# Moving the small tasks of the next tiles to other steps in the first two blocks of a fused state-space and FFN kernel

## The chip, the cores and the metric

One core of one Trainium2 chip runs the whole kernel. The metric is the device time in microseconds (us) of one execution. A difference under about 0.3% (1.4 us) can't be told from no change here.

## The reference

A sequence of 2048 tokens with 448 channels, float32 throughout. A condition vector gives six rows of 448 numbers; two layer norms are shifted and scaled by them, and both branches are gated by them.

```python
mod = (_silu(c) @ w_mod).reshape(c.shape[0], 6, 1, -1)
sa, ca, ga, sb, cb, gb = (mod[:, 0], mod[:, 1], mod[:, 2], mod[:, 3], mod[:, 4], mod[:, 5])
h = _layernorm(x, axis=-1) * (1 + ca) + sa
x = x + ga * _A_ref(h, ...)          # causal convolution along the tokens, kernel K from (A, B, C, dt), plus h * Dskip
h = _layernorm(x, axis=-1) * (1 + cb) + sb
x = x + gb * _B_ref(h, w_gate, w_up, w_down)   # (silu(h @ w_gate) * (h @ w_up)) @ w_down, 448 -> 1792 -> 448
```

## The kernel before

**Tiling.** The 2048 tokens are 16 tiles of 128, taken in 8 blocks of two tiles. Block b runs the FFN of its two tiles in 14 steps, one for each slice of 128 of the 1792 hidden channels. While it does so, the other engines prepare the two tiles of block b + 1: convolution branch, second norm, and turning the result so that channels lie on partitions. What is not ready when step 13 ends holds up the next block.

**A step f** (function `ffn`). TensorE (PE) multiplies the block's turned input (`hhi` and `hlo`, a float32 value in a high and a low part) with the gate and up weights of slice f (`gu`, also high and low): 42 pairs of matmuls on the two halves of the array. Shortly before the last pair comes `point(f)`: half of the down products of slice f - 2 and half of those of slice f - 1 (operands `wdh`, `wdl` and `phi`, `plo`, or `wd` and `p` in plain float32), and, if the table says so, a part of the convolution of a coming tile. Then ScalarE (ACT) makes `p` = silu(gate) (line 792), VectorE (DVE) multiplies with up (line 804), and ACT and DVE make `phi` (812) and `plo` (813) of it for the down products. In step 0 of a block PE reads the first four seventh-slices ("LOW") of `hhi` first; they are split from the turned tiles by ACT line 267 and DVE line 268.

**Block 0** has more to do: the weights come in for the first time. In each of its steps the SyncE queue (SP) loads gate and up of a later slice into `raw` (line 108, three buffers) and the down weights into `rawd` or `wd` (line 117), ACT and DVE split gate and up into `gu` (134, 136) and down into `wdh`, `wdl` (819, 124). For the slices 4, 6, 8, 10 and 12 (`WHOLE`) the down weights stay unsplit in block 0 and are split in block 1 (122, 124).

**The tasks.** What is done for the next tiles is cut into small tasks, one letter each, with the tile's number in the block, 0 or 1. The table `PLANS` writes them out by hand, one string for block 0, one for block 1, one for the blocks in between, one for the last but one, one for the last. Steps are parted by `;`. A task with `+` is put after the multiplication of line 804 and ahead of `phi`; one without stands at the end of the step, ahead of the split of `gu` for step f + 2; `A` and `B` go into `point(f)` on PE. Each engine runs its instructions in the order in which they are written.

The tasks that matter here: `a` h from the first norm (DVE 214, 216); `b` h times two rows (1002, DVE for block 0's tasks, GpSimd, called POOL, afterwards); `r` adds the row carried from the tile before (DVE 1007, 1008); `h` and `v` split it (`vh` ACT 1013, `vl` DVE 1019); `A` and `B` the two halves of the convolution's matmuls (operands `vh`, `vl`, `v`); `c` h times the skip row and `p` its addition to x (POOL 1024, 1027); `e` takes the carried row (ACT 1051, DVE 1052) and copies it to partition 0 by a DMA (1053); `E` adds the convolution to x (DVE 1058, 1059); `u`, `w` sums for the second norm on ACT (190, 194, with POOL 191 between them), or `m` the same on DVE (170, 171); `M` the inverse root on POOL (199, 200); `X`, `Y` the second norm (DVE 223, 225); `T` transposes blocks of 32 x 32 on DVE (255) and writes the tile to DRAM by four DMAs (257, buffer `xd`); `U` reads it back turned, by two DMAs (261, into the buffers of `raw`); `l`, `k` the last two operations of the former block's sums (DVE 840, 841); `L` loads the x tile of the block after next (91); `W4` to `W12` split the whole down weights; `o`, `O` and `d`, `R` the statistics of the first norm; `G` two matmuls with their sum for the gate row (748, 749).

The names are read by this loop in `steps`:

```python
for f, names in enumerate(plan.split(";"), -2 if b == 0 else 0):
    for name in names.split():
        n = name.lstrip("+")
        ...
        if k in "AB":
            todo.setdefault((f, "pe"), []).append((st[k], nx[q[0]]))
        else:
            todo.setdefault((f, "+") if n != name else f, []).append((of[k], q))
```

Of the kernel before, what the change touches and what calls it, by code (L numbers as in the profile page):

```python
# [34 lines left out]
ADDED = ()  # L35
WHOLE = (4, 6, 8, 10, 12)
PLANS = (
# [1131 lines left out]
```

## Time and profile before

| | before |
|---|---|
| median of 3 runs | 465.16 us (464.55 to 465.99) |
| the profiled execution's own time | 466.29 us |
| its span from first to last instruction | 464.5 us |
| busy: PE, DVE, ACT, POOL | 447.6, 294.2, 157.5, 102.7 us |
| mean granted PE clock | 1.000 |

The profiled execution took 1.79 us more than its span, and 1.13 us more than the median of the runs. All positions are us from the start of the span. Block 0 begins at 35.08, block 1 at 92.61, block 2 at 146.44, block 3 at 198.50. A timeline row reads: start, duration, engine, line, operation, output<-inputs, count, and in brackets the idle time of the engine before it and what ended that. Durations of PE rows overlap, so lengths of PE work are read from the starts.

### The profile page before, as it was taken

How to read it: one execution, taken by the hardware profiler on the slowest of the kernel's cores; microseconds unless marked ns; L12 is line 12 of the kernel's file. 1: busy time of each engine (PE TensorE's matmuls, PEld its weight loads, DVE VectorE, ACT ScalarE, POOL GpSimd, SP SyncE). 2: the span in 40 equal slices, each digit the busy share in tenths (PEclk: the TensorE clock that was granted, in tenths of full speed). 3: DMA queues.
4: the chain of work that ended last, by engine and by line, in shares of the span. 5: the costliest groups of instructions: out<-in, count | busy, mean ns of one | idle time of the engine just before them, and what ended most of it. 6: DMA issues, size and time to landing. Idle time of an engine off the chain costs nothing.

```text
span 464.5 us, 14489 instructions
## 1 busy us (share of the span) xinstructions
PE 447.6 (96%) x6335; PEld 425.9 (92%) x6335; DVE 294.2 (63%) x600; ACT 157.5 (34%) x385; POOL 102.7 (22%) x127
## 2 busy tenths in 40 slices
PE   7789999899999999999999999999999999999995
PEld 4448988689899999999999999999999999999995
DVE  4889988576865666575755666565765666344324
ACT  4877554423324222332223221332223221232211
POOL 2132331033400252033301152033301161000000
PEclk9999999999999999999999999999999999999999
DMA  8953555502031102202031202202031102202001
GB/s 305 406 218 99 193 171 180 157 5 83 2 80 42 59 25 62 61 1 82 7 79 40 66 17 61 62 16 69 11 79 34 41 4 61 61 10 74 5 1 45
DMA packets 19048, 35.71 MB, mean 77 GB/s; under 512 B 3232, under 2 KB 13088, under 8 KB 18976
## 3 DMA queue, kind: packets, MB, share of 16 engines
q1 hardware_dynamic: 18336, 34.53, 23.4%
q8 instruction: 51, 0.84, 0.8%
q10 hardware_dynamic: 640, 0.18, 0.2%
q14 instruction: 21, 0.17, 0.1%
HBM read 27.76 MB, written 6.88 MB: 75 GB/s over the span
## 4 chain that ended last, share of the span: by engine, by line
PE 81%; issue 5%; DVE 5%; ACT 3%; POOL 3%; DMA 2%; SPq 0%; POOLq 0%; DVEq 0%; ACTq 0%
PE bank L766 50%; PE dn L766 27%; DMA x<-in_A_u_dram 1%; DMA raw<-xd 1%; DVE gu L136 1%; ACT gu L134 1%; PE dn L498 1%; DVE bank L804 1%; POOL m L1002 0%; POOL rsa L200 0%; POOL v L1002 0%; PE dn L872 0%; PE dn L398 0%; DVE m L223 0%; ACT phi L812 0%
## 5 line engine op out<-in xcount | busy, mean ns | idle before, releaser
L766 PE MATMUL bank<-hhi,gu 64*128 64x256 f32 x3136 | 227.4, 275 | 3.8 <-ACT hhi L267 2.3
L766 PEld LDWEIGHTS bank<-hhi,gu 64*128 64x128 f32 x3136 | 206.9, 184 | 6.8 <-ACT hhi L267 2.8
L766 PE MATMUL bank<-hlo,gu 64*128 64x256 f32 x1568 | 134.0, 275 | 0.0
L766 PEld LDWEIGHTS bank<-hlo,gu 64*128 64x128 f32 x1568 | 119.8, 184 | 0.2
L792 ACT ACTIVATE raw<-bank 128x256 f32<-128x256 f32 x98 | 37.7, 385 | 187.3 <-PE bank L766 187.3
L804 DVE TENSOR_TENSOR bank<-raw,bank 128x256 f32<-128x256 f32 x91 | 38.8, 427 | 96.6 <-ACT raw L792 96.6
L766 PE MATMUL dn<-wdh,phi 64*128 64x448 f32 x420 | 87.2, 366 | 0.4 <-ACT phi L812 0.4
L766 PE MATMUL dn<-wdh,plo 64*128 64x448 f32 x420 | 86.2, 362 | 0.0
L766 PE MATMUL dn<-wdl,phi 64*128 64x448 f32 x420 | 85.8, 359 | 0.0
L813 DVE TENSOR_TENSOR plo<-bank,phi 128x256 fp32r<-128x256 f32 x99 | 41.9, 423 | 29.5 <-ACT phi L812 29.5
L812 ACT CAST phi<-bank 128x256 fp32r<-128x256 f32 x99 | 36.9, 373 | 61.0 <-DVE bank L804 61.0
L766 PEld LDWEIGHTS dn<-wdh,phi 64*128 64x128 f32 x420 | 48.5, 184 | 3.3 <-ACT phi L812 1.5
L766 PEld LDWEIGHTS dn<-wdh,plo 64*128 64x128 f32 x420 | 48.6, 184 | 1.8 <-DVE plo L813 0.8
L766 PEld LDWEIGHTS dn<-wdl,phi 64*128 64x128 f32 x420 | 48.9, 184 | 0.9 <-issue 0.6
L1002 POOL TENSOR_TENSOR m<-m,gm 128x448 f32<-128x448 f32 x12 | 13.9, 1155 | 78.9 <-issue 43.8
L199 POOL TENSOR_SCALAR rsa<-mva 128x2 f32<-128x2 f32 (+1 forms) x10 | 5.4, 544 | 97.7 <-DVE mva L171 91.3
L199 POOL TENSOR_SCALAR rsb<-mvb 128x1 f32<-128x1 f32 x16 | 4.3, 266 | 80.2 <-DVE mvb L171 79.7
L268 DVE TENSOR_TENSOR hlo<-raw,hhi 128x512 fp32r<-128x512 f32 (+1 forms) x28 | 16.4, 622 | 3.9 <-ACT hhi L267 1.8
L1024 POOL TENSOR_TENSOR m<-m,gd 128x448 f32<-128x448 f32 x14 | 17.0, 1212 | 7.6 <-DVE v L1002 7.6
L267 ACT CAST hhi<-raw 128x512 fp32r<-128x512 f32 (+1 forms) x28 | 14.6, 566 | 3.1 <-DMA raw<-xd 3.1
L136 DVE TENSOR_TENSOR gu<-raw,gu 128x896 fp32r<-128x896 f32 x14 | 15.1, 1080 | 0.4 <-ACT gu L134 0.4
L225 DVE SCALAR_TENSOR_TENSOR m<-m,rsb,sb 128x448 f32<-128x448 f32 x14 | 13.8, 984 | 0.8
(217 smaller groups left out, 454.5 us busy)
## 6 DMA issues: line engine op xcount, KB each, us to landing
raw<-in_B_w_gate_up_dram SPq DMA_DIRECT2D x14, 448.0 KB, 3.4
raw<-xd SPq DMA_DIRECT2D x28, 224.0 KB, 3.6
xd<-m SPq DMA_DIRECT2D x56, 56.0 KB, 1.7
x<-in_A_u_dram SPq DMA_DIRECT2D x12, 224.0 KB, 2.9
rawd<-in_B_w_down_dram SPq DMA_DIRECT2D x11, 224.0 KB, 3.5
out_dram<-x SPq DMA_DIRECT2D x11, 224.0 KB, 2.0
wm<-in_w_mod_groups_dram SPq DMA_DIRECT2D x5, 448.0 KB, 8.3
wm<-in_w_mod_groups_dram SPq DMA_DIRECT2D x5, 336.0 KB, 8.2
```

Of the source, the lines that this page charges most:

```text
L136: ve.tensor_tensor(wgu[j][:, 1], w, f32(wgu[j][:, 0]), op=OP.subtract)
L199: po.tensor_scalar(rs[:, 0:n], self.mv[:, 0:n, 1], EPS, None, op0=OP.add)
L225: ve.scalar_tensor_tensor(to, to, rs, sb, op0=OP.mult, op1=OP.add)
L267: sc.copy(hi, src)
L268: ve.tensor_tensor(lo, src, f32(hi), op=OP.subtract)
L766: done.append(pe.matmul(o, w[e], r[e], start=start, stop=stop).ins)
L792: gate_ready[:] = [sc.activation(p, ps[0][:, 0:n], AF.Silu).ins.name]
L804: ve.tensor_tensor(p if whole else ps[1][:, 0:n], p, ps[1][:, 0:n], op=OP.mult)
L812: sc.copy(hi, ps[1][:, 0:n])
L813: ve.tensor_tensor(lo, ps[1][:, 0:n], f32(hi), op=OP.subtract)
L1002: en.tensor_tensor(v, h, g, op=OP.mult)
L1024: po.tensor_tensor(h, h, gd, op=OP.mult)
```

## The change

Only two strings of the table change. No instruction is added or removed.

```diff
 PLANS = (
-    """pre: s0 ; mid: t0 R0 f s1 ; a0 +g G ; b0 t1 ; r0 h0 R1 ; v0 a1 ; A0 b1 c0 ; B0 c1 e0 p0 ; r1 h1 v1 u0 w0 +E0 M0 ; X0 Y0 p1 ; A1 T0 ; B1 E1 m1 ; +M1 X1 Y1 T1 ; +U0 ; U1 e1 L0 ; L1""",
-    """d0 R0 a0 b0 d1 R1 ; +l0 r0 h0 k0 ; +l1 v0 k1 W4 ; W6 A0 a1 b1 c0 ; B0 p0 e0 E0 c1 ; W8 r1 h1 m0 M0 p1 ; +v1 X0 Y0 L0 L1 ; W10 A1 T0 U0 ; B1 E1 m1 M1 ; W12 +X1 Y1 T1 U1 ; e1 ; ; o0 ; o1 O""",
+    """pre: s0 ; mid:  t0 R0 s1 f ; +g a0 ; b0 t1 +G ; r0 R1 h0 ; v0 ; A0 b1 c0 +a1 ; B0 c1 p0 e0 ; r1 h1 v1 +E0 u0 ; M0 A1 +w0 X0 ; p1 T0 +E1 B1 +Y0 ; m1 M1 ; Y1 +X1 T1 U0 e1 ; U1 ; L0 ; L1""",
+    """ d0 R0 a0 b0 d1 ; +l0 r0 h0 +k0 ; +l1 +k1 v0 R1 W4 ; A0 a1 b1 ; E0 B0 +e0 c0 c1 ; +W6 +p0 r1 h1 m0 M0 ; +v1 X0 L0 W8 Y0 L1 ; A1 +W10 T0 ; p1 E1 U0 B1 m1 M1 ; e1 +X1 Y1 ; +T1 ; +U1 W12 ;  ; o0 o1 O""",
```

In block 0's string the third field is step 0, in block 1's the first. Block 0: `A1` moves from step 8 to 7 and `B1`, `E1` from 9 to 8; `w0` goes behind the silu of step 7, `X0` stays at the end of step 7, `Y0` goes to step 8; `M1` comes at the end of step 9 and `X1` stays ahead of `Y1` and `T1` in step 10; `U0` goes from step 11 to the end of step 10 with `e1` (12 before), `U1` from 12 to 11; `a1` from the end of step 3 into step 4, `G` from step 0 to 1.

PE, block 0, steps 7 and 8: the six rows `dn_69<-vh`, `vl`, `v` are the second tile's `A1` (rows of the order after; `gu_686` is step 7, `gu_758` step 8).

```order
L766 MATMUL dn_68<-wd_761,p 128x448 x2
L766 MATMUL dn_69<-vh,tri 128x224 x2
L766 MATMUL dn_69<-vl,tri 128x224 x2
L766 MATMUL dn_69<-v_833,tri 128x224 x2
L766 MATMUL bank<-hhi,gu_686 128x256 x2
```

Before, the same place went from the down products straight to the last pair of step 7 (there `wd_763` is what `wd_761` is now), and these rows stood one step later:

```order
L766 MATMUL dn_68<-wd_763,p 128x448 x2
L766 MATMUL bank<-hhi,gu_686 128x256 x2
L766 MATMUL bank<-hhi,gu_760 128x256 x14
L766 MATMUL bank<-hlo,gu_760 128x256 x14
L766 MATMUL bank<-hhi,gu_760 128x256 x12
```

`A1` now stands in step 7, ahead of its last pair of gate and up matmuls.

DVE, block 0, from the end of step 8 (`T0`, the transpose, is the first row) to the end of step 11, before:

```order
L255 STREAM_TRANSPOSE m_77<-m_77 128x7x2x32
L136 TENSOR_TENSOR gu_915<-raw,gu_915 128x896
L804 TENSOR_TENSOR bank<-p,bank 128x256
L124 TENSOR_TENSOR wdl_998<-rawd_79,wdh_997 128x448
L813 TENSOR_TENSOR plo<-bank,phi 128x256
L1058 TENSOR_TENSOR x_73<-x_73,dn_69 128x448
L1059 SCALAR_TENSOR_TENSOR x_73<-dn_69,tok,x_73 128x448
L170 BN_STATS stb<-x_73 128x6
L171 BN_AGGR mvb<-stb 128x2
L136 TENSOR_TENSOR gu_995<-raw,gu_995 128x896
L804 TENSOR_TENSOR p<-p,bank 128x256
```

and after, from the product of step 8 on:

```order
L804 TENSOR_TENSOR p<-p,bank 128x256
L1058 TENSOR_TENSOR x_73<-x_73,dn_69 128x448
L1059 SCALAR_TENSOR_TENSOR x_73<-dn_69,tok,x_73 128x448
L225 SCALAR_TENSOR_TENSOR m_77<-m_77,rsb,sb 128x448
L255 STREAM_TRANSPOSE m_77<-m_77 128x7x2x32
L136 TENSOR_TENSOR gu_915<-raw,gu_915 128x896
L804 TENSOR_TENSOR bank<-p,bank 128x256
L124 TENSOR_TENSOR wdl_994<-rawd_79,wdh_993 128x448
L813 TENSOR_TENSOR plo<-bank,phi 128x256
L170 BN_STATS stb<-x_73 128x6
L171 BN_AGGR mvb<-stb 128x2
L136 TENSOR_TENSOR gu_991<-raw,gu_991 128x896
```

`E1` (1058, 1059) and `Y0` (225) have moved ahead of the first tile's transpose, and out of step 9. Behind this, after the second transpose of step 10, the row of `e1`, which stood at the end of step 12, now stands ahead of the split of step 12's `gu`:

```order
 L255 STREAM_TRANSPOSE m_77<-m_77 128x7x2x32
-L136 TENSOR_TENSOR gu_1064<-raw,gu_1064 128x896
+L1052 SCALAR_TENSOR_TENSOR run<-run,dn_69 32x448
+L136 TENSOR_TENSOR gu_1068<-raw,gu_1068 128x896
 L804 TENSOR_TENSOR bank<-p,bank 128x256
```

The queue SP, block 0, from the writes of the second tile (`xd_104`) to the loads of two x tiles, before and then after:

```order
L257 DMA xd_104<-m_77 32x2x224 x4
L117 DMA rawd_81<-in_B_w_down_dram 128x448
L261 DMA raw<-xd_103 64x896 x2
L261 DMA raw<-xd_104 64x896 x2
L1053 DMA run<-run 1x16x56
L91 DMA rawd_79<-in_A_u_dram 128x448
L91 DMA rawd_80<-in_A_u_dram 128x448
```

```order
L257 DMA xd_104<-m_77 32x2x224 x4
L261 DMA raw<-xd_103 64x896 x2
L1053 DMA run<-run 1x16x56
L117 DMA rawd_81<-in_B_w_down_dram 128x448
L261 DMA raw<-xd_104 64x896 x2
L91 DMA rawd_79<-in_A_u_dram 128x448
L91 DMA rawd_80<-in_A_u_dram 128x448
```

The read back `U0` (`xd_103`) now stands ahead of the down weights of slice 13 (`rawd_81`), the copy of the carried row stands between the two, and the read back `U1` (`xd_104`) behind both.

In block 1 the string moves `W6`, `W8`, `W10` and `W12` apart (`W12` from step 9 to 11), `T1` and `U1` one and two steps later, `k0` and `k1` ahead of `plo`, `e0` ahead of `phi` in step 4, `c1` ahead of `p0`, and `E0` ahead of `p0`: on POOL the two rows 1024 now stand ahead of 1027. Both `o` tasks stand in step 13.

## The prediction

> **What bounds the kernel now.** First the page's busy rows, then the list of waits on PE, the share of PE by block, the chain of waits at the end of block 0, and from there the timelines of the engines on it.
>
> ```profile
> PE 447.6 (96%) x6335; PEld 425.9 (92%) x6335; DVE 294.2 (63%) x600; ACT 157.5 (34%) x385; POOL 102.7 (22%) x127
> ...
> PE bank L766 <- ACT hhi L267: 2.3, 1, 2.3
> PE bank L766 <- DVE gu L136: 1.1, 2, 0.7
> ```
>
> PE is busy 96% of the span. What it waits for inside the blocks is little (total, times, longest of the list's two largest rows there), above all 2.3 us on the split of the turned tile. It is the step from block 0 to block 1; the chain there, in order of time (start, length, what):
>
> ```profile
> 86.37 0.45 SPq L261
> 86.86 5.06 DMA raw<-xd
> 91.94 0.63 ACT hhi L267
> 92.61 1.63 PE bank L766 x24
> ```
>
> PE has nothing to do from 90.35 (its last row of step 13 starts at 89.85 and lasts 0.50) to 92.61, because the second half of `U1` lands at 91.92. How the SP queue, and DVE before it, came to issue it that late:
>
> ```profile
> 76.01 0.44 SPq L117 DMA_DIRECT2D rawd<-in_B_w_down_dram  x1
> 82.69 1.74 SPq L257 DMA_DIRECT2D xd<-m  x4
> 84.47 0.43 SPq L117 DMA_DIRECT2D rawd<-in_B_w_down_dram  x1
> 85.00 2.46 SPq L261 DMA_DIRECT2D raw<-xd  x4
> 89.50 1.83 SPq L91 DMA_DIRECT2D rawd<-in_A_u_dram  x2
> ...
> 72.74 0.64 DVE L255 STREAM_TRANSPOSE m<-m 128x448 f32<-128x448 f32 x1
> 75.86 0.43 DVE L804 TENSOR_TENSOR bank<-p,bank 128x256 f32<-128x256 f32 x1 [1.50 <-ACT p L792]
> 77.07 0.61 DVE L1058 TENSOR_TENSOR x<-x,dn 128x448 f32<-128x448 f32 x1
> 79.19 1.07 DVE L136 TENSOR_TENSOR gu<-raw,gu 128x896 fp32r<-128x896 f32 x1
> 80.18 0.42 DVE L804 TENSOR_TENSOR p<-p,bank 128x256 f32<-128x256 f32 x1
> 82.02 0.65 DVE L255 STREAM_TRANSPOSE m<-m 128x448 f32<-128x448 f32 x1
> ```
>
> `T1` ends at 82.67, and from 75.86 to it DVE has no gap: it sets the time. But in front of 75.86 it waited 1.50 us for a silu. In the blocks behind, PE is the limit: by the starts of the blocks given above block 1 takes 53.83 us and block 2 52.06, so block 1 has 1.77 us over a block that PE fills, and the later blocks have nothing to give.
>
> **The change, part by part.** Nothing is added, so all is order. Rows for PE and ACT in steps 7 to 12 of block 0:
>
> ```profile
> 64.55 0.92 PE L766 MATMUL dn<-wd,p 64*128 64x448 f32 x4
> 69.92 0.27 PE L766 MATMUL dn<-vh,tri 64*128 64x224 f32 x2
> 75.06 1.09 PE L766 MATMUL bank<-hhi,gu 64*128 64x256 f32 x16
> 78.82 1.08 PE L766 MATMUL bank<-hhi,gu 64*128 64x256 f32 x16
> ...
> 65.45 0.63 DVE L1019 TENSOR_TENSOR vl<-m,vh 128x448 fp32r<-128x448 f32 x1
> 67.86 0.36 ACT L792 ACTIVATE p<-bank 128x256 f32<-128x256 f32 x1
> 79.14 0.39 ACT L792 ACTIVATE p<-bank 128x256 f32<-128x256 f32 x1 [1.60 <-PE bank L766]
> 81.16 0.57 ACT L819 CAST wdh<-rawd 128x448 fp32r<-128x448 f32 x1 [0.80 <-DMA rawd<-in_B_w_down_dram]
> ...
> 87.72 0.53 ACT L1051 COPY run<-dn 32x448 f32<-32x448 f32 x1
> 88.27 0.63 DVE L1052 SCALAR_TENSOR_TENSOR run<-run,dn 32x448 f32<-32x448 f32 x1 [0.79 <-ACT run L1051]
> ```
>
> *`A1` in step 7.* PE reaches the place when the down products are issued, 64.55 + 0.40 (the distance of such a row to the next) = 64.95. The operand `vl` ends at 65.45 + 0.63 = 66.08; the DVE tasks ahead of it stay in order. So the change adds a wait of 1.15 us on PE, and the last pair of step 7, the silu of step 7 and step 8 queue behind it. The matmuls themselves take 0.32 (69.92 to 70.24 where the next rows start). Step 8 starts at about 66.45 instead of 64.95.
>
> *`w0` behind the silu of step 7.* Before, that silu stood behind both sums and started at 67.86; now it can start 0.3 after step 7 ends (as 79.14 follows 78.82), at 66.75. That returns 1.1 us to DVE, whose product of step 7, `X0` and the split of `gu` for step 9 come earlier; PE's shorter wait on `gu` in the list (0.4) goes. One step of PE takes 3.75 (75.06 to 78.82). Steps 8 to 10 from 66.45, with `B1` (0.32) still in step 8: 66.45 + 3 x 3.75 + 0.32 = 78.0, against 78.82. So the added wait is paid back by step 10, with 0.8 over.
>
> *`E1`, `Y0` ahead of `T0`, out of step 9.* `E1` is two operations like the one at 77.07, together 1.3 us. In step 8 it fills the gap of 1.50; `T0` ends about 0.85 later (74.25 for 73.4), which nothing waits for but the SP queue. In step 9 DVE now has 1.3 less: the product of step 9 starts at 75.25 (behind the split of `gu`), then 0.34 + 0.53 + 0.34 to the statistics, 0.75 for these, 1.0 for the split: 78.2. The silu of step 10 comes at 78.0 + 0.32. So the product of step 10 starts at 78.4 instead of 80.18, and `T1`, which ends 2.49 after it (80.18 to 82.67), ends at 80.9 instead of 82.67: **1.8 us sooner**.
>
> *`U0`, `e1`, `U1` on SP.* From 80.9: the four writes 1.74, ends 82.7; `U0` two times 0.55, 83.8; the copy of the carried row 0.53 and the down weights 0.43, 84.85; `U1` at 84.95 and 85.5, against 86.37 and 86.86. Both queues it is moved past are in that sum: the second half goes out **1.36 sooner**, since two smaller DMAs now stand between the read backs.
>
> *`e1` in step 10: what it holds.* On ACT its copy stands behind the split of `rawd` (line 819), which at 81.16 waited for its DMA, and on DVE row 1052 then stands ahead of the split of step 12's `gu`. The load was issued at 76.01 and took 5.1 us; now SP issues it about 0.5 later, as `T0`'s writes are later:
>
> ```profile
> rawd<-in_B_w_down_dram SPq DMA_DIRECT2D x1, 224.0 KB, 5.1
> raw<-xd SPq DMA_DIRECT2D x1, 224.0 KB, 3.5
> raw<-xd SPq DMA_DIRECT2D x1, 224.0 KB, 3.8
> raw<-xd SPq DMA_DIRECT2D x1, 224.0 KB, 4.2
> raw<-xd SPq DMA_DIRECT2D x1, 224.0 KB, 5.1
> raw<-xd SPq DMA_DIRECT2D x2, 224.0 KB, 3.4
> ```
>
> The columns are size and us from issue to landing. With 5.1 the weights land at 81.65, with 3.5 at 80.0. At worst, then: 81.65 + 0.55 (819) + 0.53 (1051) + 0.63 (1052) = 83.4, and the split of step 12's `gu` ends at 84.45; PE wants it at about 83.1 (step 12 would start 0.8 to 1.2 early, at 81.05; two thirds of its gate and up come first, 2.05 with the slow start behind plain float32 products). So PE waits up to 1.3, step 13 ends at about 90.8, or 90.0 with the early landing. `U1`, which overwrites that `raw` buffer, is free to go at 84.45, ahead of its turn at 84.95.
>
> *Landing.* The first four rows on `raw<-xd` are `U0` and `U1` in order: they landed at 88.5, 89.3, 90.6 and 91.9, about 1 us apart, behind 224 KB of down weights. The last is `U1` in block 1, where the queue is empty: 3.4. After the change `U0` would land at 86.3 and 87.1, the weights at 88.0, `U1` at 89.0 and 90.0. Bounds: 85.5 + 3.4 = 88.9, and 85.5 + 5.1 = 90.6. I take 90.1, from the spacing. With 0.63 for the split and 0.06 of handing over, block 1 starts at **90.8 instead of 92.61: 1.8 us less** (1.3 to 2.6, the latter where both PE and the landing are early).
>
> One thing behind `U1` is new: the two x loads (448 KB) no longer wait for the carried row but follow at once, at 86.1 instead of 89.5. Whether they slow `U1` no row shows. [...]
>
> *Block 1.* The rows of its dearest place, the starts of PE's steps 6 and 7 and the wait between them:
>
> ```profile
> 116.08 1.14 PE L766 MATMUL bank<-hhi,gu 64*128 64x256 f32 x16
> 120.53 1.07 PE L766 MATMUL bank<-hhi,gu 64*128 64x256 f32 x16
> ...
> 117.27 0.62 DVE L1058 TENSOR_TENSOR rawd<-rawd,dn 128x448 f32<-128x448 f32 x1 [2.08 <-POOL rawd L1027]
> 119.40 0.47 PE L766 MATMUL dn<-wdh,phi 64*128 64x448 f32 x2 [0.44 <-ACT phi L812]
> ```
>
> `E0` waited 2.08 us for `p0` on POOL, held the product of the next step, and PE lost 0.85 (116.08 to 120.53 is 4.45, where the later blocks take 3.60 for a step). Now `E0` stands ahead of `p0` and waits for no POOL row: +0.85. Against it: `e0` ahead of `phi` makes ACT wait for row 1052 before it can issue the copy and cast `phi`, about 0.2 on PE in step 5; `k0`, `k1` ahead of `plo` delay `plo` by one such operation (0.54) where PE takes it as soon as it is made, at most 0.4 by step 3. Net **0.25**, between -0.4 and 0.85. `T1` and `U1` are one step later there: `U1` would land at about 144.8, the split wants it at 144.87, PE at 146.44, so nothing is lost while the landing stays under 4.5 us.
>
> `a1`, `G`, `R1` in steps 0 to 5 of block 0: up to 0.5 of PE's two waits on `gu` (1.1 in the list) goes, but `vl` in step 6 then sets the pace, so I count nothing. The spread splits and the `o` tasks lie beside PE, on a DVE that is busy 63% and an ACT that is busy 34% of the span; if that cover were short, a split costs its 0.57 on ACT.
>
> Sum: 1.8 + 0.25 = **2.05 us** on the profiled execution: span 464.5 to 462.45, its own time 466.29 to 464.24. Its own time stands 1.13 above the median of the runs, so the runs' median goes from 465.16 to **463.1**.
>
> **The rivals.**
>
> *Little is gained (within 0.3%, that is 1.4 us).* Either the x loads share the DMA engines with `U1`: 448 KB more at the rate that spaces the halves (224 KB a us) is 2 us, `U1` lands at 92 and block 1 starts as late as before; or the wait for `vl` costs PE more than it gets back, `T1` comes only 0.75 sooner and `U1` 0.3 sooner. For it speaks that SP has more between `T1` and `U1` now; against it, the gap of 1.50 that `E1` fills. Time: 0.25 to 1.0 saved, 464.2 to 464.9.
>
> *Slower, by `e1`.* PE's step 12, SP's copy of the carried row and with it `U1` all queue behind one load. Each us that the weights of slice 11 land later than 81.65 puts 1 us on both paths. The saving is used up when they land 2.05 later, at 83.7, 7.2 us after the issue; the loss passes 1.4 us at 85.1. Against it: no such load in the block took over 5.1. Time with a landing of 9 us: 466.8.
>
> *More is gained.* The weights land in 3.5, `U1` in 3.4, and block 1 keeps its 0.85: 90.0 for the start of block 1, 2.6 + 0.85 = 3.45, 461.7.
>
> **How the numbers follow.** Forecast (1.4 to 2.9 saved) 0.50; more 0.13; little (0 to 1.4) 0.26; lost 0.11, of which 0.07 by over 1.4 us. So faster 0.63, same 0.30, slower 0.07. The range from 461.6 to 465.2 takes in the bounds of landing and block 1 (3.45 down to nothing) and leaves out the loss and part of the largest gain.
>
> **What would show it.** PE in step 7 waits about 1.1 us on `vl`; `T1` near 80.9, `U0` ahead of 84, `U1` at 85 to 85.5 and landed near 90; the wait on line 267 down from 2.3 to under 1; a wait of DVE for the copy of 1051 in step 10; PE's wait on `phi` in block 1 gone. Wrong it would be if `T1` does not move, if `U1` takes over 5 us, if the load of slice 11 lands after 82, or if a wait on line 267 turns up at 146.

## The result, and the profile after

The changed kernel takes 463.11 us (median of 20 runs, 462.38 to 465.58) against 465.83 for the kernel before in the same sessions (20 runs, 464.40 to 467.93). The ratio is 0.9945, 95% interval 0.9933 to 0.9957: 2.6 us less, with 2.0 and 3.1 as ends.

The profiled execution has a span of 461.0 us for 464.5. Its list of PE's waits inside the blocks (total, times, longest):

```profile
PE bank L766 <- DVE gu L136: 0.7, 1, 0.7
PE dn L766 <- ACT gu L134: 0.7, 1, 0.7
PE dn L766 <- DVE plo L813: 0.4, 1, 0.4
...
PE bank L766 <- ACT hhi L267: 0.4, 1, 0.4
PE dn L766 <- DVE vl L1019: 0.3, 1, 0.3
```

PE's wait on line 267, the split of the turned tile, is down from 2.3 to 0.4. In its place stand short ones. The timelines of DVE and SP at the end of block 0:

```profile
75.87 1.07 DVE L136 TENSOR_TENSOR gu<-raw,gu 128x896 fp32r<-128x896 f32 x1
77.38 0.42 DVE L804 TENSOR_TENSOR p<-p,bank 128x256 f32<-128x256 f32 x1 [0.44 <-ACT p L792]
77.72 0.68 DVE L223 SCALAR_TENSOR_TENSOR m<-x,mvb,cbw 128x448 f32<-128x448 f32 x1
78.50 0.69 DVE L225 SCALAR_TENSOR_TENSOR m<-m,rsb,sb 128x448 f32<-128x448 f32 x1
79.22 0.65 DVE L255 STREAM_TRANSPOSE m<-m 128x448 f32<-128x448 f32 x1
81.17 0.63 DVE L1052 SCALAR_TENSOR_TENSOR run<-run,dn 32x448 f32<-32x448 f32 x1 [1.30 <-ACT run L1051]
...
79.90 1.74 SPq L257 DMA_DIRECT2D xd<-m  x4
81.74 1.14 SPq L261 DMA_DIRECT2D raw<-xd  x2
82.97 0.54 SPq L1053 DMA_DIRECT2D run<-run  x1
83.56 0.59 SPq L117 DMA_DIRECT2D rawd<-in_B_w_down_dram  x1
84.33 1.09 SPq L261 DMA_DIRECT2D raw<-xd  x2
85.46 1.06 SPq L91 DMA_DIRECT2D rawd<-in_A_u_dram  x2
```

`T1` ends at 79.87. Ahead of the products of steps 9 and 10 together DVE waits 0.44 us for a silu where it waited 1.50 before (for step 9's, at 73.92, it no longer waits). `U0` and `U1` go out apart. The chain of waits there:

```profile
84.33 0.45 SPq L261
84.82 4.20 DMA raw<-xd
...
89.10 0.63 ACT hhi L267
89.77 1.68 PE bank L766 x24
```

The second half of `U1` still ends last, at 89.02, but now only just. Block 0 starts at 33.80 here and at 35.08 before. The code ahead of it is the same, and over the profiles of this study its start lies anywhere from 33.19 to 35.08, so positions are compared from the start of block 0:

| from the start of block 0, us | before | after |
|---|---|---|
| `T1` ends | 47.59 | 46.07 |
| second half of `U1` issued, and the time to its landing | 51.78, 5.06 | 51.02, 4.20 |
| block 1 starts | 57.53 | 55.97 |
| length of block 1 | 53.83 | 53.69 |

The two blocks have 1.70 us less between them. Of the 3.47 between the spans 1.28 is the start of block 0, and 0.49 lies behind block 1 (318.06 to 317.57), where the code is the same; over the profiles that stretch takes 317.5 to 319.0. So a pair of profiles shows 1.7 us for the change where the timing shows 2.6. Where the rest is comes out of the experiments.

### The profile page after: what moved, and what is told of

Same layout as the page of the kernel before. It is cut to its first block, busy times and chain, and to the rows that moved or that the text cites. A ratio compares the mean times of both kernels' runs of the same rounds, so it can differ in the third digit from the quotient of the medians.

```text
span 461.0 us, 14489 instructions
## 1 busy us (share of the span) xinstructions
PE 446.8 (97%) x6335; PEld 425.9 (92%) x6335; DVE 294.0 (64%) x600; ACT 157.4 (34%) x385; POOL 103.4 (22%) x127
## 4 chain that ended last, share of the span: by engine, by line
PE 83%; DMA 8%; DVE 3%; ACT 3%; issue 1%; SPq 1%; POOL 0%; ACTq 0%; POOLq 0%
PE bank L766 53%; PE dn L766 29%; DMA wm<-in_w_mod_groups_dram 4%; DMA raw<-in_B_w_gate_up_dram 2%; DMA rawd<-in_B_w_down_dram 1%; DMA raw<-xd 1%; DMA vec<-in_c_log_dt_dram 1%; ACT gu L134 1%; DVE gu L136 0%; DVE bank L804 0%; PE dn L872 0%; ACT run L1051 0%; ACT phi L812 0%; DVE x L1059 0%; DVE run L1052 0%
## 5 line engine op out<-in xcount | busy, mean ns | idle before, releaser
L199 POOL TENSOR_SCALAR rsa<-mva 128x2 f32<-128x2 f32 (+1 forms) x10 | 6.4, 638 | 97.8 <-DVE mva L171 91.9
L1027 POOL TENSOR_TENSOR x<-m,x 128x448 f32<-128x448 f32 x10 | 13.8, 1380 | 4.4 <-DVE x L1059 4.1
```

Source lines behind the costliest of these rows:

```text
L199: po.tensor_scalar(rs[:, 0:n], self.mv[:, 0:n, 1], EPS, None, op0=OP.add)
L1027: po.tensor_tensor(xs[i], vs[i][0], xs[i], op=OP.add)
```

## The experiments

All on one table: the ratio to the kernel before timed beside it, and from one profile each the end of `T1`, the issue and flight of the second half of `U1`, PE's wait on line 267, and the lengths of blocks 0 and 1. The last column counts the runs whose mean granted PE clock was 0.996 or less; it is read at the end of this section; for before it covers the runs timed beside the experiments.

| kernel | ratio (95%) | `T1` | `U1` | wait | block 0 | block 1 | clock |
|---|---|---|---|---|---|---|---|
| before | 1 | 47.59 | 51.78 + 5.1 | 2.26 | 57.53 | 53.83 | 43 of 82 |
| after | 0.9945 (0.9933 to 0.9957) | 46.07 | 51.02 + 4.2 | 0.38 | 55.97 | 53.69 | 0 of 20 |
| queue_only | 1.0009 (0.9990 to 1.0028) | 47.53 | 51.88 + 4.8 | 2.16 | 57.39 | 55.34 | 6 of 10 |
| compute_only | 0.9957 (0.9940 to 0.9975) | 46.08 | 50.29 + 4.8 | 1.44 | 55.82 | 53.77 | 2 of 10 |
| e1_late_held | 0.9963 (0.9947 to 0.9979) | 46.10 | 50.45 + 5.1 | 1.81 | 56.21 | 53.87 | 3 of 10 |
| e1_late_loads | 0.9979 (0.9961 to 0.9997) | 46.15 | 50.50 + 5.5 | 2.26 | 56.72 | 53.80 | 5 of 10 |
| block0_only | 0.9966 (0.9950 to 0.9982) | 46.13 | 51.06 + 3.9 | 0.38 | 55.70 | 53.71 | 0 of 10 |
| block1_only | 0.9996 (0.9972 to 1.0019) | 47.60 | 51.80 + 5.1 | 2.24 | 57.56 | 55.23 | 5 of 10 |
| a1_back | one run | 46.14 | 51.07 + 5.2 | 2.65 | 57.04 | 54.97 | 1 of 1 |
| u0_early | 0.9939 (0.9915 to 0.9963) | 46.13 | 50.10 + 4.6 | 0.91 | 55.36 | 53.81 | 0 of 7 |
| w0_only | 0.9997 (0.9978 to 1.0016) | 46.85 | 51.05 + 5.2 | 2.41 | 56.98 | 55.24 | 8 of 12 |
| w0_back | 0.9964 (0.9946 to 0.9983) | 46.08 | 51.01 + 5.3 | 1.54 | 57.10 | 53.69 | 1 of 10 |
| p0_behind_E0 | 0.9985 (0.9966 to 1.0005) | 47.55 | 51.74 + 5.2 | 2.37 | 57.63 | 52.93 | 5 of 10 |
| best | 0.9927 (0.9908 to 0.9946) | 46.24 | 50.96 + 4.5 | 1.59 | 56.14 | 53.09 | 0 of 6 |

**Is it the sooner `T1`, or the order of SP's queue?** queue_only has block 0 of the kernel before, with the read backs a step earlier, and the changed block 1. compute_only is the changed kernel with the order of before in the queue.

```diff
 queue_only, block 0 (from before)
-... +M1 X1 Y1 T1 ; +U0 ; U1 e1 L0 ; L1
+... +M1 X1 Y1 T1 U0 ; U1 ; e1 L0 ; L1
 compute_only, block 0 (from after)
-... Y1 +X1 T1 U0 e1 ; U1 ; L0 ; L1
+... Y1 +X1 T1 ; +U0 ; U1 e1 L0 ; L1
```

> Block 0 of the kernel before with only U0 (end of step 10) and U1 (step 11) sooner; e1 and all arithmetic tasks where they stood before; block 1 as in the changed kernel. Theory (T1 on DVE decides when U1 can go): T1 ends as before, about 47.6 us after the start of block 0, U1 goes out at most 0.2 sooner, block 0 takes 57.3 (57.5 before, 56.0 in the changed kernel). Rival (the order of the queue is what gave the time): block 0 at 56.5 or less.

> The changed kernel, but U0, U1 and e1 back in steps 11 and 12 where they stood before. Theory (the sooner T1 is what gave the time): T1 ends about 46.1 after the start of block 0 instead of 47.6, and block 0 takes 55.6 to 56.0, like the changed kernel's 56.0 or less. Rival (the queue's order gave it): block 0 at 57 or more.

The queue alone gains nothing, the sooner `T1` alone nearly all. With the old queue `U1` even goes out 0.73 sooner than in the changed kernel; it lands at 55.1 for 55.2. In queue_only the chain of waits runs over ACT: the down weights, now behind `U0`, stand ahead of the split of the turned tile, and ACT ran its three rows in the written order, behind a wait of 3.17 us for the weights (88.69, 89.28 and 89.83).

```profile
88.69 0.56 ACT L819 CAST wdh<-rawd 128x448 fp32r<-128x448 f32 x1 [3.17 <-DMA rawd<-in_B_w_down_dram]
89.28 0.52 ACT L1051 COPY run<-dn 32x448 f32<-32x448 f32 x1
89.83 1.14 ACT L267 CAST hhi<-raw 128x512 fp32r<-128x512 f32 x2
```

It cost hardly anything, though: the second half of `U1` landed at 90.28, and its split, the second of the two casts, began at 90.35.

**What does `e1` in step 10 cost, and the x loads behind `U1`?** `e1` goes back to step 12, once ahead of the x loads, which then wait for it, once behind them.

```diff
 e1_late_held, block 0 (from after)
-... T1 U0 e1 ; U1 ; L0 ; L1
+... T1 U0 ; U1 ; e1 L0 ; L1
 e1_late_loads, block 0 (from after)
+... T1 U0 ; U1 L0 L1 ; e1 ;
```

> The changed kernel with e1 alone put back to step 12, ahead of the x loads, so these wait behind the carried row as before. Theory (e1 in step 10 holds DVE and PE): DVE's wait of 1.30 us on ACT's copy and PE's 0.71 on gu in step 12 go, U1 is issued 0.9 sooner relative to T1's end, block 0 takes 55.05 instead of 55.97. Rival (the wait fell into slack): block 0 stays at 55.9 to 56.0.

> As the kernel with e1 alone late, but the two x loads stand right behind U1, ahead of e1. If what is queued behind takes nothing from U1: its second half lands as long after its issue as there (within 0.2) and block 0 is the same, 55.05. If the engines are shared: U1 lands 0.5 to 2 us later, block 0 at 55.5 to 57.

The first one's forecast missed: DVE's wait of 1.30 and PE's wait on `gu` went and PE was done with block 0 by 54.4, 1.2 earlier, but then it stood 1.81 for `U1`. The hold by `e1` lies in slack; the landing ends last. In the second kernel, with the loads right behind `U1`, `U1` takes 0.5 longer than in the first. That is the direction of sharing, but one and the same queue gave 3.9 in block0_only and 5.3 in w0_back, so it isn't shown.

**Which block?**

```diff
 block0_only: block 0's string as after, block 1's as before
 block1_only: block 0's string as before, block 1's as after
```

> Block 0's string of the change, block 1's string as before. Theory: block 0 takes 56.0 (57.5 before), block 1 53.8, as before; the whole is 1.6 us less than before, ratio 0.9966, since block 1's string gave only 0.15. Rival (block 1's string gives what the sum of the two blocks in the profiles leaves open): less than 1.2 saved, ratio over 0.9975.

> Block 1's string of the change, block 0's string as before. Theory: E0 no longer waits for POOL (0.85 less in step 6), but k0 ahead of plo costs 0.65 in step 2 and e0 ahead of phi 0.45 in step 5; block 0 57.5, block 1 53.7, no difference that can be told. Rival: block 1 a whole 0.85 shorter, 53.0.

As expected: block 0's string has the gain, block 1's none that shows.

**What brings `T1` forward: `A1`, `B1`, `E1` a step sooner, or `w0` behind the silu?** Each is undone in the changed kernel, and `w0` alone is put into the kernel before.

```diff
 a1_back, block 0 (from after)
-... M0 A1 +w0 X0 ; p1 T0 +E1 B1 +Y0 ; m1 M1 ; ...
+... M0 +w0 X0 ; A1 p1 T0 +Y0 ; B1 E1 m1 M1 ; ...
 w0_back, block 0 (from after)
-... +E0 u0 ; M0 A1 +w0 X0 ; ...
+... +E0 u0 w0 ; M0 A1 X0 ; ...
 w0_only, block 0 (from before)
-... u0 w0 +E0 M0 ; X0 Y0 p1 ; ...
+... u0 +E0 ; +w0 M0 X0 Y0 p1 ; ...
```

> The changed kernel with A1 back in step 8 and B1, E1, m1, M1 in step 9 (w0, X0, Y0, T0 and the queue as changed). Theory (E1 out of step 9 is what brings T1 forward): T1 ends 47.2 to 47.6 after the start of block 0 instead of 46.1, block 0 takes 57.0 or more. Rival (w0 behind the silu brought it): T1 stays under 46.5 and block 0 at 56.0 or less.

> The changed kernel with w0 back ahead of the silu of step 7. Theory now (either move is enough, the second falls into slack): the silu of step 7 comes about 1 us later, but DVE's gap of 1.03 us ahead of the product of step 8 takes it up: T1 still ends 46.0 to 46.3 after the start of block 0, block 0 within 0.5 of the changed kernel's 56.0. Rival (w0 alone brought T1 forward): T1 at 47 or later, block 0 at 56.9 or more.

> The kernel before with one edit: w0 moved behind the silu of step 7 (two instructions of ACT change places). Theory now (the silu of step 7 was the late one; with it in time DVE loses no 1.2 us there, and E1 may stay in step 9): T1 ends 46.1 to 46.4 after the start of block 0 instead of 47.6, block 0 takes 55.8 to 56.5, ratio 0.996 to 0.998. Rival (E1 has to leave step 9 as well): T1 at 47.2 or later and block 0 at 57.2 or more, ratio 0.999 to 1.001.

The theory behind a1_back fell: `T1` stays at 46.14 with `A1` and `E1` back. It stays at 46.08 with `w0` back too. Either move alone keeps nearly all of the 1.5 us within the changed order; `w0` alone on the kernel before gives half of it (0.74), so something else of the new order (`a1`, `G`, `Y0` at other steps) carries the other half, and which isn't settled. Both kernels that undo a part have the `T1`, queue and issue of the changed kernel, and still a block 0 about 1.1 longer. The chains of a1_back and of w0_back name what differs:

```profile
84.67 5.22 DMA raw<-xd
```

```profile
84.52 5.35 DMA raw<-xd
```

The same DMA at the same place flies 4.20 in the changed kernel's profile, 3.9 in block0_only's. What goes with the longer flight is in the last section: a single packet of 16 KB in another queue, of 0.96 to 1.32 us, which in a1_back and w0_back stands ahead of the last rows of the flight, and in the other two starts only at 87.58 and 87.98, with no such rows behind it. Whether it falls there by chance or by the order one profile of each can't say.

**More of the same.** `U0` ahead of the second transpose; block 1 with `p0` behind `E0` alone; and both together, with `k0` and `e0` back behind `plo`.

```diff
 u0_early, block 0 (from after)
-... Y1 +X1 T1 U0 e1 ; U1 ; L0 ; L1
+... Y1 +U0 +X1 T1 ; U1 ; e1 L0 ; L1
 p0_behind_E0, block 1 (from before)
-... B0 p0 e0 E0 c1 ; W8 r1 ...
+... B0 e0 E0 c1 ; W8 p0 r1 ...
 best: u0_early, and in block 1 (from after)
-... +l0 r0 h0 +k0 ; ... ; E0 B0 +e0 c0 c1 ; ...
+... +l0 r0 h0 k0 ; ... ; B0 e0 E0 c0 c1 ; ...
```

> The changed kernel with U0 ahead of T1 (in step 10, so that the first read back does not queue between the second tile's write and its read back), and e1 back in step 12 ahead of the x loads. Theory (U1's landing is set by the bytes that SP's queue has to move after T1: about 224 KB a us): only 672 KB instead of 1120 KB are left after T1, U1 lands 1.5 to 2 sooner, at 53.2 to 53.7 after the start of block 0; then PE is the bound, whose step 13 ends at 54.4 there; block 0 takes 54.4 to 54.6, PE's wait on line 267 is under 0.2. Rival (each read back has a fixed time of its own from T1 on): U1 lands at 55 as in the kernel with e1 late, block 0 at 55.8 to 56.2.

> The kernel before with one edit in block 1: p0 moved behind E0 (from step 4 to step 5). Theory: DVE's E0 waits for no POOL row, the 0.85 that PE lost in step 6 goes, block 1 takes 53.0 instead of 53.8, ratio 0.998. Rival (the wait was cover for something that is late next, as the statistics m0, which now wait for p0): block 1 53.6 or more.

> The changed kernel with U0 ahead of T1 and e1 late (as in u0_early), and in block 1 k0 and e0 put back behind plo, while E0 stays ahead of p0. Theory: block 1 loses neither 0.65 in step 2 nor 0.45 in step 5 and takes 52.6 to 52.8 (53.7 in the changed kernel); block 0 55.4 as in u0_early, give or take 0.5; ratio to the kernel before 0.992 to 0.993. Rival (k0 and e0 were put there because something later needs them early): block 1 at 53.3 or more, ratio 0.994 or more.

u0_early sends `U1` 0.9 sooner, but of the expected 54.4 to 54.6 for block 0 it reaches 55.36, since PE again waits 0.91 for a flight of 4.6. p0_behind_E0 does in block 1 what was expected (52.93). best has 53.09 there for the expected 52.6 to 52.8. Its median of 461.76 (461.12 to 461.95, 6 runs) is the lowest of all, 3.3 us under the kernel before. It wasn't timed beside the changed kernel, and the intervals of the two ratios overlap, so that it beats that one as well is likely but not shown.

**The rest of the gain: the clock behind the wait.** In queue_only, block1_only, a1_back and w0_only block 1 came out 1.3 to 1.7 us longer than in after. Its busy rows by microsecond, of queue_only and then of before (length, busy times, and behind POOL's the granted PE clock as a share of full speed):

```profile
90.00:91.00 1.00, 0.00 (x0) 0.00 (x0) 0.97 (x2) 0.97 (x3) 0.00 (x0) 1.00 0.00 0
91.00:92.00 1.00, 0.98 (x10) 0.98 (x12) 1.00 (x3) 0.37 (x1) 0.00 (x0) 0.59 0.02 4
92.00:93.00 1.00, 1.00 (x14) 1.00 (x14) 0.81 (x3) 0.33 (x2) 0.00 (x0) 0.50 0.66 177
93.00:94.00 1.00, 1.00 (x10) 0.96 (x10) 0.87 (x3) 1.00 (x3) 0.00 (x0) 0.50 0.79 290
94.00:95.00 1.00, 1.00 (x6) 0.45 (x4) 0.65 (x2) 0.00 (x0) 0.00 (x0) 0.70 0.00 0
95.00:96.00 1.00, 1.00 (x18) 0.96 (x16) 0.00 (x0) 0.00 (x0) 0.00 (x0) 1.00 0.00 0
```

```profile
92.00:93.00 1.00, 0.39 (x6) 0.39 (x8) 0.41 (x1) 0.95 (x2) 0.00 (x0) 1.00 0.93 351
93.00:94.00 1.00, 1.00 (x22) 1.00 (x22) 0.97 (x3) 0.00 (x0) 0.00 (x0) 1.00 0.06 17
94.00:95.00 1.00, 1.00 (x12) 0.55 (x10) 0.83 (x4) 0.82 (x4) 0.00 (x0) 1.00 0.00 0
```

When PE comes back from its wait of 2.16 in queue_only, its clock is at half for 3.4 us: the shortfalls of the four rows, 0.41, 0.50, 0.50 and 0.30, add up to 1.71 us lost. Before's own profile, with a wait of 2.26, has none of it. Over all 14 profiles: of the seven with a wait of 2.16 or more four show the drop, each with 1.70 or 1.71 lost; of the seven with 1.81 or less none. Taken off, block 1 is 53.3 to 53.6 in those four, no longer than elsewhere.

What parts the four from the other three is where the wait falls. The trace keeps the moments at which the granted clock changes. In queue_only it is full from 5.85 to 91.18, half to 94.60, full again to 463.24: stretches of 85.33, 3.41 and 368.64 us, which are 25, 1 and 108 times 3.413. In all 14 profiles the stretches between two changes are whole multiples of 3.413 us (457.39 us, 134 of them, in before; 453.97, 133, in after), so in these the clock changed only on a grid of that step. The grid lies differently in each execution: it has a boundary at 92.07 in before and at 91.18 in queue_only. Laid over PE's wait, it gives:

| profile | wait | most of it within one 3.413 us of the grid | clock behind it |
|---|---|---|---|
| w0_only | 2.41 | 2.41 | half |
| a1_back | 2.65 | 2.35 | half |
| block1_only | 2.24 | 2.24 | half |
| queue_only | 2.16 | 2.16 | half |
| e1_late_held | 1.81 | 1.81 | full |
| before | 2.26 | 1.72 | full |
| p0_behind_E0 | 2.37 | 1.38 | full |
| e1_late_loads | 2.26 | 1.32 | full |

The other six waits are of 1.59 or less. So the clock fell where 2.16 us or more of one step of the grid passed idle, and it did not fall at 1.81 or less. Three longer waits that a boundary of the grid cut in two (before, p0_behind_E0, e1_late_loads: 2.26, 2.37 and 2.26 us, with 1.72, 1.38 and 1.32 in one step) were spared. An estimate from these figures: a wait of 2.26 that falls anywhere on the grid has 1.81 of it in one step in 60% of the places, 2.16 in 40%. The runs of the kernel before had the low clock in 43 of 82, 52%.

The mean clock of every run shows this without a profile. Of the 82 runs of the kernel before beside these experiments 43 had a mean clock of 0.996 or less and a median of 466.24; the other 39 had 464.72. None of the changed kernel's 20 runs was that low. (The split isn't clean: a drop at the very end of the program also takes a little off the mean; the profiles of e1_late_held and p0_behind_E0 have 0.996 from that alone.) By and large the share in the table's last column goes with the wait.

So the time of the kernel before is a mixture. Against its runs with the full clock the change saves 464.72 - 463.11 = 1.6 us, close to what the profiles show (1.70). These runs are of other sessions than those of the changed kernel, and their medians by session are 464.42, 464.69 and 465.28, so the 1.6 may be 1.3 to 2.2. The other 0.9 or so is an estimate, 43 of 82 times 1.71 us: the drop that no longer comes. The same sum fits elsewhere: by runs at 0.997 and above compute_only saves 465.28 - 463.34 = 1.9 within its session (profiles 1.77) and p0_behind_E0 464.42 - 463.41 = 1.0 (profiles: 0.9 in block 1). block0_only doesn't fit: 0.3 by its runs, 1.95 by its profile, whose execution took 463.32 in a range from 463.03 to 465.02. No kernel was run that changes the wait and nothing else, so the tie between wait and clock rests on these 14 profiles, one of each kernel.

## Why the prediction was right, and where only by its sum

Forecast 463.1, measured 463.11. The mechanism of block 0, a sooner `T1` and with it a sooner `U1`, held. That the number is met so closely is luck. The forecast took 2.05 from 465.16, the median of the first three runs of the kernel before; all 20 beside the changed kernel gave 465.83, and the difference of the medians is 2.72. The saving of 2.05 is made of parts that were not all right.

- *`T1`, 1.8 sooner.* 1.5 (47.59 to 46.07). For the silus of steps 7, 8, 9 and 10 DVE waited 1.18, 0, 1.50 and 0 us before, and 0.17, 1.03, 0 and 0.44 us now. The row at 68.25 is of before, the others are of after; those with 1.50 and 0.44 stand further up:

```profile
68.25 0.43 DVE L804 TENSOR_TENSOR bank<-p,bank 128x256 f32<-128x256 f32 x1 [1.18 <-ACT p L792]
...
65.75 0.43 DVE L804 TENSOR_TENSOR bank<-p,bank 128x256 f32<-128x256 f32 x1 [0.17 <-ACT p L792]
69.79 0.42 DVE L804 TENSOR_TENSOR p<-p,bank 128x256 f32<-128x256 f32 x1 [1.03 <-ACT p L792]
76.96 0.38 ACT L792 ACTIVATE p<-bank 128x256 f32<-128x256 f32 x1 [1.38 <-PE bank L766]
```

The gap of 1.50 in front of step 9's product closed, as said. The missing 0.3 is a slip in the forecast's sum: it let the product of step 10 start 0.08 behind the start of its silu (78.32 and 78.4), but the silu has to end first, and the rows have 0.42 between the two starts (76.96 and 77.38). By its own rows `T1` would have come 1.4 sooner. That `E1` out of step 9 does it is wrong as the only cause (a1_back); the new gap of 1.03 is the slack into which a part that is undone can fall.
- *`A1` in step 7, a wait of 1.15 on `vl`.* Right in size, though the list of waits names only 0.3. By the forecast's own measure PE reached the place at 63.05 + 0.40 = 63.45 and `vl` ended at 64.57, 1.12 later; the next pair starts at 64.94, 1.49 behind the place for the 1.50 forecast. Part of it was spent ahead of the row on `vh`, which ACT made until 63.91. It is paid back as said: the row that the forecast put at 78.0, 42.92 from the start of block 0, starts at 42.76 (43.74 before).

```profile
63.05 1.01 PE L766 MATMUL dn<-wd,p 64*128 64x448 f32 x4
63.97 0.37 PE L766 MATMUL dn<-vh,tri 64*128 64x224 f32 x2
64.63 0.37 PE L766 MATMUL dn<-vl,tri 64*128 64x224 f32 x2 [0.29 <-DVE vl L1019]
64.83 0.28 PE L766 MATMUL dn<-v,tri 64*128 64x224 f32 x2
64.94 1.10 PE L766 MATMUL bank<-hhi,gu 64*128 64x256 f32 x16
...
63.35 0.56 ACT L1013 CAST vh<-m 128x448 fp32r<-128x448 f32 x1 [1.30 <-DVE m L1007]
63.95 0.62 DVE L1019 TENSOR_TENSOR vl<-m,vh 128x448 fp32r<-128x448 f32 x1
```

- *SP: second half of `U1` 1.36 sooner.* 0.76. Of the 0.6 missing 0.27 is `T1`; the rest are gaps between SP's rows and the weights' issue of 0.59 that was put at 0.43.
- *Landing 4.6 after the issue, at 55.0 from the start of block 0.* 4.20, at 55.2. The quicker flight made up for most of the late issue, and that was luck too (3.9 to 5.3 for the same queue); block 1 starts 1.56 sooner for 1.8.
- *`e1`: PE waits up to 1.3 if the weights are late.* They landed at 80.0, 4.66 after the issue, between the bounds; DVE waited 1.30 for the copy and PE 0.7 on `gu`. It cost next to nothing on the path, as PE was done with step 13 only 0.38 before the operands came.
- *Block 1, 0.25 gained.* 0.14 by the profiles. `E0` ahead of `p0` gave its 0.85, in rows: step 6 went from 4.45 to 3.60 (113.93 to 117.53). `k0` ahead of `plo` took 0.66 in step 2 (0.4 at most in the forecast; the wait is below), `e0` ahead of `phi` 0.46 in step 5 (0.2), and 0.44 came back in steps 0 and 3.

```profile
101.22 0.47 PE L766 MATMUL dn<-wdh,plo 64*128 64x448 f32 x2 [0.45 <-DVE plo L813]
```

- *The rivals.* The x loads did not bring block 1 back to its old start. The forecast counts nothing for them behind `U1`, and no run shows that they take nothing: e1_late_loads had a flight of 5.5 and a block 0 of 56.72 with them right behind, e1_late_held 5.1 and 56.21 with them held, and kernels with the queue of the changed one lie from 3.9 to 5.3. The weights did not come late. Nothing waited on line 267 at the end of block 1.
- *What failed: a step that was not there.* PE's wait on line 267 was priced at its own length. By the profiles above it also put PE's clock at risk of 1.71 us, and 43 of the 82 runs of the kernel before had the low clock. The steps that were there add up to 1.7, 0.35 under the forecast; the drop that went adds about 0.9. So the saving was some 0.6 larger than the forecast's 2.05, and the median still fell on the forecast because the median of the three runs that it took off from lies 0.67 below that of the 20.

## What to carry to other kernels

A wait of TensorE was followed here by a loss on top of its length: of 1.70 or 1.71 us in four of the seven profiles with a wait of 2.16 to 2.65 us, and in none of the seven with 1.81 or less. Look at the granted clock in the microseconds behind such a wait, and in the mean clock of all runs: with the low clock in 43 of the 82 runs of the kernel before, one profile of each kernel gave 1.7 us for a difference that the timing put at 2.6, and the step from a wait of 2.26 to one of 0.38 was worth about 0.9 us on top of the shorter blocks, by the estimate above.

In a hand-written order, moving a task was free where its engine had a gap on the path that ends last (`T1` at 46.14 in a1_back for 46.07, with a gap of 1.03 in the changed kernel), and cost what stood behind it in that order elsewhere: `E0` behind a POOL task cost a step 0.85 us, `k0` ahead of `plo` 0.66. Where the last wait was for a DMA, freeing the compute engines ahead of it bought nothing (e1_late_held: PE done 1.2 us sooner, block 0 56.21 for 55.97). A sooner issue did (u0_early: 0.9 sooner, 55.36), and block 0 was shorter where the flight was (block0_only and w0_back, issued at 51.06 and 51.01: 3.9 and 5.3 us, 55.70 and 57.10).

## What the runs showed of the hardware

Besides the clock: the flight of one and the same 224 KB read back, the second half of `U1`, was 3.9 to 5.3 us at the same place of the same queue (after, block0_only, a1_back, w0_back), and 3.9 to 5.5 over all profiles. In u0_early about 2 us of it are a thin tail. There `U1` was issued by 83.94 and landed at 88.5; the bytes by half microseconds (last columns: share of the DMA engines, GB/s):

```profile
85.50:86.00 0.50, 0.50 (x12) 0.49 (x10) 0.00 (x1) 0.47 (x2) 0.00 (x0) 1.00 1.29 370
86.00:86.50 0.50, 0.50 (x8) 0.47 (x6) 0.50 (x1) 0.50 (x1) 0.00 (x0) 1.00 0.69 194
86.50:87.00 0.50, 0.50 (x7) 0.22 (x4) 0.47 (x2) 0.11 (x1) 0.00 (x0) 1.00 0.05 7
87.00:87.50 0.50, 0.50 (x10) 0.41 (x8) 0.35 (x1) 0.00 (x0) 0.00 (x0) 1.00 0.09 14
87.50:88.00 0.50, 0.50 (x12) 0.50 (x12) 0.00 (x0) 0.00 (x0) 0.00 (x0) 1.00 0.08 21
88.00:88.50 0.50, 0.29 (x6) 0.09 (x2) 0.00 (x0) 0.00 (x0) 0.00 (x0) 1.00 0.16 26
```

The bulk had moved by 86.5. Behind it the trace has five packets of 3584 B, rows of `U1`; the other bytes are the copy of the carried row (224 B each, from 87.85) and the x loads (1792 B each, from 88.43). The last four rows run one behind the other, from 87.07, 87.45, 87.81 and 87.94 to 88.08, at a share of the engines (0.09 and 0.08) near one of sixteen. What stood ahead of them in time is a single packet of 16 KB in another queue. Its lines in the list of DMA queues, of u0_early at 85.83 and of after at 87.58 (packets, MB, share of 16 engines in a window of 0.02 us, so that 395% is 1.26 us):

```profile
q8 instruction: 1, 0.02, 395.0%
q8 instruction: 1, 0.02, 446.6%
```

In u0_early it ends at 87.09, as the first of the four rows starts. In 12 of the 14 profiles the same stands in the flight: such a packet of 0.96 to 1.32 us, as it ends a row of 0.39, then one of 0.36, then the rest one behind the other (in before the packet from 89.18 to 90.50, the last rows from 90.49, 90.86, 91.22 and 91.36 to 91.50); these flights are 4.5 to 5.5 us. In after and block0_only it starts at 87.58 and 87.98, with no such rows behind it, and their flights, 4.20 and 3.90, are the two shortest. The trace gives the queue's name and the packet's size and time. Whether the packet holds up the rows, and what sets its moment, was not tried.
